# Attention, token choice and expert layers on one core: new layout for the choice's matmuls, moved waits, five operations on GpSimd, one round of key sums folded in

## The chip, the cores and the metric

The program runs on one core of a Trainium2 chip. The metric is the device time of one execution in microseconds (us): the median of three runs. A core has five engines with queues of their own, called here PE (matmuls; its weight loads are shown as PEld), DVE (vector), ACT (scalar), POOL (GpSimd) and SP (here it only starts transfers).

## What is computed

```python
scores = scale * q @ k.T; scores = cap*tanh(scores/cap)        # 8 batches, 12 heads, 448 keys, 64 wide
attn = softmax(scores); x = attn @ v                           # x: 3584 tokens x 768
logits = x @ w_gate                                            # 8 experts
for idx in argsort(-logits.flatten()):                         # greedy, highest logit first
    tok, e = idx // 8, idx % 8
    if assigned[tok] < 0 and counts[e] < 448: assigned[tok] = e; counts[e] += 1
out[assigned == e] = relu(x[assigned == e] @ w1[e]) @ w2[e]    # 768 -> 1024 -> 768
```

All in float32; every expert takes exactly 448 tokens.

## The kernel before, in words

**Attention (`attention`, from the start to about 349 us).** 24 steps g, one for each batch and group of four heads. A step makes scores for 128 keys at a time (`qk`), ACT does tanh and exp, PE multiplies with the values (`av`, `avrem` for the last 64 keys). The row sums of the exponentials, which are needed for the division and for the gate, come from DVE adds over the key tiles (`esum`, L158: parts e1, e2, o1, o2, and r for the last 64 keys) and a matmul with a column of ones (`rnd`, L191). For the last step of the last batch the part r is not added by DVE: four more matmuls (L297) sum the last 64 keys straight from the exponentials. `logit` transposes the gate sums, divides them and keeps the 8 logits of each token.

**Choice (`Routing`).** The greedy choice is done expert by expert: in each of 8 passes the expert that fills up first is found with its 448 tokens. For that, `propose_a` and `propose_b` write each token's best open expert and its logit as three numbers (VA, VB, VC) and a key (K1, K2). `search` then finds the 448th value for each expert: three stages A, B, C (`select`) with 5, 6 and 5 rounds. A round compares 224 proposals with three thresholds (two on DVE, one on ACT), sums the counts with a 4-column matmul (L464), and DVE sets the next thresholds (L468, L471). `finalise` numbers the chosen tokens: `oj` and `oh` are one-hot in the high and low part of the position, `rj` is `oj` times the row number, and four matmuls (L581) with `oh` as weights put every row number in its place. DVE folds the result (`ek`, `ev`), a small matmul (L588) spreads it, and `idx` is what the gather reads. The first pass runs with no other work but the last transposes of attention's result (L37, multiplied by the reciprocal row sums on POOL, L45, and written to `xs` in memory). The other passes run between the matmuls of the experts.

**Experts (`ffn_all`).** For each of 8 experts: `gather` asks for 448 rows of `xs` in four transfers (L721, POOL), PE transposes them (`tx`, L728, for expert 0; `xtr`, L737, for the others, six blocks at fixed places in the expert before), ACT and DVE split them in a high and a low part, and PE does the first layer (L766: 8 groups f of 18 matmuls, 144 in all) and the second (L793: 176). 320 matmuls are one expert. Each of these 320 is a *tick*. The choice is a Python generator whose `yield n` says after how many ticks its next piece is put into the engines' queues; a negative number names a place counted from the start. The queues are in order, so a piece put in too early makes the matmuls behind it wait. `s.hA` is the distance from the compares to the matmul L464, `s.hB` the one from L464 to the next compares. PE is kept working by `warm` matmuls (128x128, results not used) while the first gather is under way: 18 of them after L588 of the first choice, and four between the transposes.

Of the kernel before, what the change touches and what calls it, by code (L numbers as in the profile page):

```python
# [17 lines left out]
def attention(nc, tc, c1, xp, pM, q, k, v, cap, w_gate, xs, L1, ident, on_logits, on_turn, NDEF, xd, setup):  # L18
# [3 lines left out]
    B,H,S,D=q.shape  # L22
# [29 lines left out]
    with ExitStack() as ctx:  # L52
# [228 lines left out]
        g=N-1; b=B-1  # L281
        rnd(b,rB[1][0],False,False); rnd(b,rB[1][1],False,True)
        logit_in(b)
        av(g,0,2); av(g,1,0)
        esum(g,'o1')
        part=logit(b,0,2,final=False)
        esum(g,'o2')
        av(g,1,1)
        avrem(g)
        av_out(g,0)  # L290
        av(g,1,2)
        rnd(b,rB[2][0],True,False)
        av_out(g,1)
        ps=misc[b]
        for gt,kind,a,h in rB[2][0]:
            o,t=h//2%2,h%2; w=64*(t^o)
            nc.tensor.matmul(ps[gt*32:gt*32+32,:S],ones[w:w+64,a,:],ev(g,6)[w:w+64,o,:],start=False,stop=False)  # L297
        rnd(b,rB[2][1],False,True)
# [7 lines left out]
TA=0  # L306
EW=1; WT=4
FMAX=3.4028234e38
class Routing:
# [4 lines left out]
    def setup(s):  # L314
# [23 lines left out]
        nc.gpsimd.tensor_copy(s.e8m,s.e8c)  # L338
        s.ihi=t("ihi",[CP,16,NC],I16)
        nc.gpsimd.iota(s.ihi,[[1,16],[0,NC]],base=0,channel_multiplier=0)  # L340
        s.ilo=t("ilo",[CP,28,NC],I16)
# [55 lines left out]
    def propose_a(s,L,c0,c1):  # L397
# [13 lines left out]
        v.tensor_tensor(w("VA"),w("P"),bc(w("At")),op=ALU.mult)  # L411
    def propose_b(s,c0,c1,parts=(0,1,2,3)):
        T=s.T; n=c1-c0; v=s.nc.vector
        w=lambda k:T[k][:,c0:c1]
        bc=lambda a:a.unsqueeze(2).broadcast_to([112,n,8])
        for x in parts:
            if x==0:
                v.tensor_scalar(w("b"),w("u"),10,4095,op0=ALU.arith_shift_right,op1=ALU.bitwise_and)
                v.tensor_scalar(w("c"),w("u"),1023,None,op0=ALU.bitwise_and)
            if x==1:  # L420
                v.tensor_scalar(w("Bt"),w("b"),-2048.0,2.0**-12,op0=ALU.add,op1=ALU.mult)
                v.tensor_scalar(w("Ct"),w("c"),1024.0,2.0**-22,op0=ALU.add,op1=ALU.mult)
            if x==2:
                v.tensor_tensor(w("VB"),w("P"),bc(w("Bt")),op=ALU.mult)
                v.tensor_tensor(w("VC"),w("P"),bc(w("Ct")),op=ALU.mult)
            if x==3:
                v.tensor_tensor(w("K1"),w("At"),w("Bt"),op=ALU.add)
                v.scalar_tensor_tensor(w("K2"),w("kk"),2.0**-25,w("Ct"),op0=ALU.mult,op1=ALU.add)
    def psum(s):
# [19 lines left out]
    def select(s,wp,Vt,ab,mid=None,post=None):  # L449
        nc=s.nc; v=nc.vector  # L450
        NV=s.NV; steps=s.steps[ab]; H=s.H[ab]; C=s.C[ab]
        th=[s.T0[ab][:,k:k+1] for k in range(3)]
        for i in range(steps):
            cd=s.cds[s.nd%3]; s.nd+=1
            o=wp.tile([128,s.NX],BF16,name="cmpA",bufs=1)
            with nc.allow_low_precision(reason="integers up to 256 are exact in bfloat16"):
                for k in range(s.na,3): nc.scalar.activation(o,Vt,AF.Sign,bias=th[k],scale=-1.0,accum_out=cd[:,k:k+1])
                for k in range(s.na):
                    o=wp.tile([128,NV],BF16,name="cmpD",bufs=2)
                    with s.tc.issue_after(s.hold) if s.hold else nullcontext(): v.tensor_scalar(o,Vt[:,:NV],th[k],None,op0=ALU.is_lt,op1=ALU.add,accum_out=cd[:,k:k+1])  # L460
            if mid and i<len(mid): mid[i]()
            s.pos='A'; yield s.hA; s.pos=''
            ps=s.psum()
            nc.tensor.matmul(ps[:,:4],s.bo,cd,start=True,stop=True)  # L464
            if post and i==(3 if s.cur==0 else 0): post()
            t0=wp.tile([128,1],F32,name="th",bufs=6)
            fl=wp.tile([128,4],F32,name="fl",bufs=3)
            v.scalar_tensor_tensor(fl,ps[:,:4],s.lim,H[:,i,0:4],op0=ALU.is_le,op1=ALU.mult,accum_out=t0)  # L468
            if i+1<steps:
                nt=wp.tile([128,1],F32,name="nt",bufs=2)  # L470
                v.tensor_scalar(H[:,i+1,3:6],C[:,i+1,:],t0,None,op0=ALU.add,op1=ALU.add,accum_out=nt) if ACF else v.tensor_scalar(H[:,i+1,3:6],C[:,i+1,:],t0,None,op0=ALU.add)  # L471
                th=[t0,H[:,i+1,4:5],H[:,i+1,5:6]]
            if i==steps-1:
                s.tA=t0
                if ab=="C": s.row(s.tA)
            s.pos='B'; yield s.hB; s.pos=''
    def search(s,wp,turned=()):
        nc=s.nc; v=nc.vector
        post=None
        if turned:  # L480
            for h in range(s.NC//16):
                if ("VA",h) not in turned: s.turn("VA",h)
            late=[lambda x=x: s.propose_b(s.NC-4,s.NC,(x,)) for x in range(4)]
            post=lambda: s.flips(s.pm.tile([128,512],F32,name="psM"))
        else: late,post=s.turns()
# [58 lines left out]
    def finalise(s,wp,L,update):  # L544
# [26 lines left out]
        v.tensor_tensor(oj,s.ilo,hi[:,1,:].unsqueeze(1).broadcast_to([112,28,NC]),op=ALU.is_equal)  # L571
        oh=s.oh=wp.tile([112,16,NC],F16,name="oh",bufs=1)
        v.tensor_tensor(oh,s.ihi,hi[:,0,:].unsqueeze(1).broadcast_to([112,16,NC]),op=ALU.is_equal)
        rj=wp.tile([112,28,NC],F16,name="rj",bufs=1)
        v.tensor_tensor(rj,oj,s.idc.unsqueeze(1).broadcast_to([112,28,NC]),op=ALU.mult)
        yield 18
        ps=s.psum()
        oc=oh.rearrange("p r c -> p (r c)")
        G=NC//8
        for g in range(G):  # L580
            nc.tensor.matmul(ps[:,:224].rearrange("p (j k) -> p j k",k=8),oc[:,g::G],rj[:,:,g::G],start=(g==0),stop=(g==G-1))  # L581
        ek=wp.tile([128,28,8],F16,name="ek",bufs=1); ev=wp.tile([128,28],F16,name="ev",bufs=1)
        v.tensor_tensor(ek,ps[:,:224].rearrange("p (j k) -> p j k",k=8),s.mk.unsqueeze(1).broadcast_to([128,28,8]),op=ALU.mult)
        with nc.allow_low_precision(reason="one term of each sum is not zero"):
            v.tensor_reduce(ev,ek,axis=AX.X,op=ALU.add)
        yield 4
        ps=s.psum()
# [7 lines left out]
        if update:  # L595
          with s.tc.issue_after(mark.ins) if s.cur==0 else nullcontext():
            z=wp.tile([112,1],F32,name="zz")
            v.tensor_scalar(z,rj[:,0,0:1],0.0,None,op0=ALU.mult)
            v.scalar_tensor_tensor(gt,m[:,0,:],z,m[:,1,:],op0=ALU.add,op1=ALU.add)
# [27 lines left out]
def ffn_all(nc, tc, ctx, rt, xs, w1, w2, out, ident, E, wp, deferred, xctx, gen):  # L627
# [125 lines left out]
    def ffn1(p,f,work):  # L753
# [160 lines left out]
```

## Time and profile before

| | |
|---|---|
| median of 3 runs | 939.32 us (938.67 to 940.23) |
| the profiled execution | 939.89 us, of which the span is 938.1 us |
| PE busy | 898.5 us, 96% of the span |
| DVE, ACT, POOL busy | 586.3, 574.1, 345.2 us |
| end of attention / first expert matmul / last expert matmul starts | 349, 399.2, 929.8 us |

A PE that is busy for 96% bounds the kernel, but a busy PE is not one at its peak: in the last matmuls of a stage it works at one of two clocks, and matmuls with results that nobody uses count as busy. So the shares are read by stage, and in each stage the wait that ends last.

### The profile page before, as it was taken

To read this page: it belongs to the slowest core of one execution; us is meant where nothing else is said; L and a number is where in the kernel's file an instruction comes from. 1 tells how busy PE (TensorE), PEld (TensorE's weight loads), DVE (VectorE), ACT (ScalarE), POOL (GpSimd) and SP (SyncE) were. 2 spreads that over 40 slices of the span, in tenths; PEclk is the share of its full clock that TensorE was granted. 3 is DMA by queue.
4 is the path that set the end of the run, shared out by engine and by line. 5 is a ranking of instruction groups with operands and counts; after the bars stand their busy time and mean duration, and the time that the engine had idled before them with its cause. 6 is when DMAs were issued, how large, how long until landed. Compare 5 with 4: busy or idle time off the path is not lost.

```text
span 938.1 us, 16367 instructions
## 1 busy us (share of the span) xinstructions
PE 898.5 (96%) x5770; PEld 619.8 (66%) x5770; DVE 586.3 (62%) x1980; ACT 574.1 (61%) x795; POOL 345.2 (37%) x469
## 2 busy tenths in 40 slices
PE   5899999999999996799999999999999999999996
PEld 1223333333323235688889989989989989999996
DVE  4779797989888767766665666656656654231210
ACT  6999898999999947274373472562662651532520
POOL 5100000000000007573483493392492683764831
PEclk9999999999999999799999999999999999999998
DMA  8677775856785006760921814516417407426301
GB/s 136 116 142 130 153 136 123 145 121 122 189 166 98 1 20 238 215 211 1 317 71 45 298 46 137 212 41 195 161 32 228 144 18 245 144 57 232 99 9 50
DMA packets 291699, 123.01 MB, mean 131 GB/s; under 512 B 224768, under 2 KB 275712, under 8 KB 291104
## 3 DMA queue, kind: packets, MB, share of 16 engines
q1 hardware_dynamic: 285104, 99.70, 42.7%
q0 software_dynamic: 4656, 22.02, 6.5%
q8 instruction: 45, 0.74, 0.3%
q10 hardware_dynamic: 1856, 0.23, 0.2%
q14 instruction: 38, 0.31, 0.1%
HBM read 97.15 MB, written 24.77 MB: 130 GB/s over the span
## 4 chain that ended last, share of the span: by engine, by line
PE 77%; issue 8%; ACT 5%; POOL 4%; DVE 4%; DMA 2%; ACTq 0%; POOLq 0%; DVEq 0%
PE psH L766 22%; PE psH L793 19%; PE psA L172 11%; PE psS L144 11%; PE psM L191 4%; ACT e L150 3%; PE psS L149 2%; DMA xg<-xs,idx 2%; PE psX L737 2%; PE psA L179 2%; PE psM L37 1%; ACT e L154 1%; DVE cmpD L460 1%; POOL out_dram L778 1%; POOL xn L45 1%
## 5 line engine op out<-in xcount | busy, mean ns | idle before, releaser
L793 PE MATMUL psH<-w2h,hh 128*128 128x384 f32 x896 | 249.5, 344 | 0.0
L793 PE MATMUL psH<-w2l,hh 128*128 128x384 f32 x512 | 175.1, 342 | 0.0
L150 ACT ACTIVATE e<-psS,s 128x896 f32<-128x896 f32 x168 | 161.0, 1000 | 20.4 <-PE psS L144 12.6
L793 PEld LDWEIGHTS psH<-w2h,hh 128*128 128x128 f32 x896 | 163.1, 189 | 0.8
L154 ACT ACTIVATE e<-e,bias,capt 128x1792 f32<-128x1792 f32 (+2 forms) x74 | 154.2, 2083 | 2.5
L45 POOL TENSOR_TENSOR xn<-raw,rin 112x512 f32<-112x512 f32 x24 | 24.4, 1048 | 323.5 <-ACT raw L42 321.7
L766 PE MATMUL psH<-xgh,w1h 128*128 128x448 f32 x384 | 142.6, 371 | 0.3 <-ACT xgh L742 0.3
L766 PE MATMUL psH<-xgh,w1l 128*128 128x448 f32 x384 | 142.3, 371 | 0.0
L766 PE MATMUL psH<-xgl,w1h 128*128 128x448 f32 x384 | 142.1, 370 | 0.0
L144 PE MATMUL psS<-tq,tk 64*64 64x448 f32 x1152 | 127.8, 559 | 9.0 <-DVE rcap L229 6.0
L172 PE MATMUL psA<-e,nv 128*64 128x448 f32 x576 | 124.1, 552 | 0.0
L698 POOL TENSOR_TENSOR w2l<-w2r,w2h 128x768 fp32r<-128x768 f32 x64 | 117.8, 1841 | 12.8 <-ACT w2h L694 12.8
L698 POOL TENSOR_TENSOR w1l<-w1r,w1h 128x768 fp32r<-128x768 f32 x62 | 114.0, 1840 | 20.1 <-ACT w1h L694 15.5
L158 DVE TENSOR_TENSOR es<-es,e 128x896 f32<-128x896 f32 (+1 forms) x94 | 101.9, 1084 | 1.9
L773 DVE SCALAR_TENSOR_TENSOR hh<-psH,hh 128x64 fp32r<-128x64 f32 (+1 forms) x128 | 44.1, 387 | 93.6 <-ACT hh L771 93.2
L799 ACT ACTIVATE on<-psH 128x384 f32<-128x384 f32 x48 | 23.6, 491 | 122.4 <-PE psH L793 122.4
L793 PEld LDWEIGHTS psH<-w2l,hh 128*128 128x128 f32 x512 | 96.7, 189 | 0.0
L172 PEld LDWEIGHTS psA<-e,nv 128*64 128x64 f32 x576 | 34.9, 136 | 83.8 <-issue 69.2
L144 PEld LDWEIGHTS psS<-tq,tk 64*64 64x64 f32 x1152 | 37.0, 134 | 80.1 <-issue 48.8
L766 PEld LDWEIGHTS psH<-xgh,w1h 128*128 128x128 f32 x384 | 72.5, 189 | 5.9 <-ACT xgh L742 0.5
L766 PEld LDWEIGHTS psH<-xgh,w1l 128*128 128x128 f32 x384 | 72.5, 189 | 5.3
L771 ACT ACTIVATE hh<-psH 128x448 fp32r<-128x448 f32 x64 | 34.8, 543 | 67.3 <-PE psH L766 63.1
(255 smaller groups left out, 1256.6 us busy)
## 6 DMA issues: line engine op xcount, KB each, us to landing
w1r<-in_moe_w_dram SPq DMA_DIRECT2D x64, 384.0 KB, 3.7
w2r<-in_moe_w_dram SPq DMA_DIRECT2D x32, 768.0 KB, 7.5
k<-in_k_dram SPq DMA_DIRECT2D x92, 112.0 KB, 2.8
q<-in_q_dram SPq DMA_DIRECT2D x92, 112.0 KB, 2.9
nv<-in_v_dram SPq DMA_DIRECT2D x72, 128.0 KB, 3.0
xs<-xn SPq DMA_DIRECT2D x4, 1344.0 KB, 7.0
xs<-xn SPq DMA_DIRECT2D x4, 896.0 KB, 5.2
xd<-xT SPq DMA_DIRECT2D x2, 1344.0 KB, 6.3
```

The lines of the kernel that those rows point to most:

```text
L45: (nc.gpsimd if late else nc.vector).tensor_tensor(xn[b][:,:,h0:h0+3:2,:],src, rin[b][:,:,2*p:2*p+2].unsqueeze(3).broadcast_to([CP,NJ,2,D] ...
L144: for c in range(2): nc.tensor.matmul(ps[c*64:c*64+64,h,:S],tks[g,0][hp,o,u*128+c*64:u*128+c*64+64],tks[g,1][hp,o,:],start=True,stop=True)
L150: nc.scalar.activation(ev(g,r),ps[:,:,:S],AF.Tanh,scale=s1)
L154: nc.scalar.activation(e,e,AF.Exp,scale=capt,bias=bias)
L158: t=es_t[g]; add=lambda o,a,b: nc.vector.tensor_tensor(o,a,b,op=ALU.add)
L172: nc.tensor.matmul(avp[g,o][h*64:h*64+64,:S],z[:,j,HG*h+o,:],ev(g,3*o+j)[:,h,:],start=(j==0),stop=(o==1 and j==2 and op is None))
L191: nc.tensor.matmul(ps[g*32:g*32+32,:S],lhs,rhs,start=first,stop=last)
L698: (eng or nc.gpsimd).tensor_tensor(view(l),r,view(h).bitcast(F32),op=ALU.subtract)
L766: nc.tensor.matmul(ps[:,:C],a[:,c,:],b[:,c,:],start=(m==0),stop=(m==DC*3-1)); m+=1
L771: nc.scalar.activation(h[:,:C],ps[:,:C],AF.Relu)
L773: nc.vector.scalar_tensor_tensor(h[:,d:d+b-a],ps[:,a:b],0.0,h[:,a:b].bitcast(F32),op0=ALU.max,op1=ALU.subtract)
L793: nc.tensor.matmul(ps[:,:HD],h[:,f,a:a+128],spl[p,2,hf,f//2][w][:,f%2,:],start=(m==0),stop=(m==nm-1))
```

## The change

Six groups of edits.

- Row sums of the last step: o1 and o2 are added ahead of `logit_in`, r is added by DVE too, ahead of `logit`, and the four matmuls L297 go; the second copy of attention's result (`av_out(g,1)`) is issued ahead of the sums' matmuls.
- The fields b and c of a proposal are computed in `propose_a`. The rest of `propose_b` for the last four columns of the first pass goes to POOL, in the first round of stage A, where DVE did it two operations at a time in four rounds; only K2 stays on DVE, in the third round.
- The choice's matmuls: `oh` and the index table are laid out as 4 groups x 16 x 8, so that the 128 weights of a matmul are neighbours in memory, where they were every fourth element; the moving columns are runs of eight neighbours instead of every fourth element. The row number is multiplied into the weights (`oi`, 512 elements) instead of into `oj` (896).
- `yield 8` in place of `yield 4` ahead of the matmul L588.
- During the second pass (`s.cur==1`) the distance from compares to L464 is 8 ticks, or, for less than 20 ticks after the end of a first-layer group, 12 less those ticks and at least 6. It was 7. The first compares of that pass stand at tick 16 instead of 18.
- 12 warm matmuls after the first choice instead of 18.

```diff
         rnd(b,rB[1][0],False,False); rnd(b,rB[1][1],False,True)
+        esum(g,'o1')
+        av(g,0,2); av(g,1,0)
+        esum(g,'o2')
         logit_in(b)
-        av(g,0,2); av(g,1,0)
-        esum(g,'o1')
+        esum(g,'r')
         part=logit(b,0,2,final=False)
-        esum(g,'o2')
         av(g,1,1)
         avrem(g)
         av_out(g,0)
         av(g,1,2)
+        av_out(g,1)
         rnd(b,rB[2][0],True,False)
-        av_out(g,1)
-        ps=misc[b]
-        for gt,kind,a,h in rB[2][0]:
-            o,t=h//2%2,h%2; w=64*(t^o)
-            nc.tensor.matmul(ps[gt*32:gt*32+32,:S],ones[w:w+64,a,:],ev(g,6)[w:w+64,o,:],start=False,stop=False)
         rnd(b,rB[2][1],False,True)
...
+        v.tensor_scalar(w("b"),w("u"),10,4095,op0=ALU.arith_shift_right,op1=ALU.bitwise_and)
+        v.tensor_scalar(w("c"),w("u"),1023,None,op0=ALU.bitwise_and)
+    def propose_b(s,c0,c1,v=None):
+        T=s.T; n=c1-c0; v=v or s.nc.vector
...
+        v.tensor_scalar(w("Bt"),w("b"),-2048.0,2.0**-12,op0=ALU.add,op1=ALU.mult)
+        v.tensor_scalar(w("Ct"),w("c"),1024.0,2.0**-22,op0=ALU.add,op1=ALU.mult)
+        v.tensor_tensor(w("VB"),w("P"),bc(w("Bt")),op=ALU.mult)
+        v.tensor_tensor(w("VC"),w("P"),bc(w("Ct")),op=ALU.mult)
+        v.tensor_tensor(w("K1"),w("At"),w("Bt"),op=ALU.add)
+        if v is s.nc.vector: s.key(c0,c1)
+    def key(s,c0,c1):
+        w=lambda k:s.T[k][:,c0:c1]
+        s.nc.vector.scalar_tensor_tensor(w("K2"),w("kk"),2.0**-25,w("Ct"),op0=ALU.mult,op1=ALU.add)
...
-            s.pos='A'; yield s.hA; s.pos=''
+            s.pos='A'; yield max(6,12-s.since()) if s.cur==1 and s.since()<20 else s.hA+1*(s.cur==1); s.pos=''
...
-            late=[lambda x=x: s.propose_b(s.NC-4,s.NC,(x,)) for x in range(4)]
+            late=[lambda: s.propose_b(s.NC-4,s.NC,PB(nc)),lambda: None,lambda: s.key(s.NC-4,s.NC)]
...
-        oh=s.oh=wp.tile([112,16,NC],F16,name="oh",bufs=1)
-        v.tensor_tensor(oh,s.ihi,hi[:,0,:].unsqueeze(1).broadcast_to([112,16,NC]),op=ALU.is_equal)
-        rj=wp.tile([112,28,NC],F16,name="rj",bufs=1)
-        v.tensor_tensor(rj,oj,s.idc.unsqueeze(1).broadcast_to([112,28,NC]),op=ALU.mult)
+        G=NC//8
+        wide=lambda t: t.rearrange("p (g k) -> p g k",k=8).unsqueeze(2).broadcast_to([112,G,16,8])
+        oh=wp.tile([112,G,16,8],F16,name="oh",bufs=1)
+        v.tensor_tensor(oh,s.ihi,wide(hi[:,0,:]),op=ALU.is_equal)
+        oi=wp.tile([112,G,16,8],F16,name="oi",bufs=1)
+        v.tensor_tensor(oi,oh,wide(s.idc),op=ALU.mult)
         yield 18
         ps=s.psum()
-        oc=oh.rearrange("p r c -> p (r c)")
-        G=NC//8
         for g in range(G):
-            nc.tensor.matmul(ps[:,:224].rearrange("p (j k) -> p j k",k=8),oc[:,g::G],rj[:,:,g::G],start=(g==0),stop=(g==G-1))
+            nc.tensor.matmul(ps[:,:224].rearrange("p (j k) -> p j k",k=8),oi[:,g].rearrange("p r k -> p (r k)"),oj[:,:,g*8:g*8+8],start=(g==0),stop=(g==G-1))
...
-        yield 4
+        yield 8
         ps=s.psum()
         s.selmm=nc.tensor.matmul(ps[:,:28],s.sel,ev,start=True,stop=True)
...
+    rt.warm=warm; rt.since=lambda: now[0]-end[0]
...
+        end[0]=now[0]
         h=hh[p][:,f,:]
         nc.scalar.activation(h[:,:C],ps[:,:C],AF.Relu)
...
-    WG=3; NW=18; WJ=4
+    WG=3; NW=12; WJ=4
...
-    hint[0]=18
+    hint[0]=16
     tx(0,4)
```

Three places show what moves in the queues.

DVE at the end of attention, before (es: row sums, e: exponentials, lg: gate sums, xT: attention's result):

```order
L158 TENSOR_TENSOR es<-es,e_3106 128x896
L195 COPY lg<-psM 128x448
L158 TENSOR_TENSOR es<-e_3106,e_3138 128x896
L208 RECIPROCAL rg_3194<-psM 112x32
L215 TENSOR_TENSOR lt_3196<-psM,rg_3194 112x256
L223 TENSOR_REDUCE lt_3198<-lt_3196 112x4x8
L224 COPY rin<-rg_3194 112x4x4x2
L158 TENSOR_TENSOR es<-es,e_3138 128x896
L184 COPY xT<-psA 128x448 x2
```

and with the change:

```order
L158 TENSOR_TENSOR es<-es,e_3106 128x896
L158 TENSOR_TENSOR es<-e_3106,e_3138 128x896
L158 TENSOR_TENSOR es<-es,e_3138 128x896
L195 COPY lg<-psM 128x448
L158 TENSOR_TENSOR es<-es,e_3138 64x2x448
L158 TENSOR_TENSOR es<-es,e_3138 64x896
L208 RECIPROCAL rg_3197<-psM 112x32
L215 TENSOR_TENSOR lt_3199<-psM,rg_3197 112x256
L223 TENSOR_REDUCE lt_3201<-lt_3199 112x4x8
L224 COPY rin<-rg_3197 112x4x4x2
L184 COPY xT<-psA 128x448 x2
```

Two adds stand ahead of the copy L195 now, and two half adds (64 partitions each) are new behind it. On PE, four matmuls fewer stand behind the copies L184.

PE in the choice of expert 1, before (the second layer of expert 0 runs around it; hh: its input, ev: the folded row numbers):

```order
L581 LDWEIGHTS oh
L581 MATMUL psR<-rj,oh 128x224
L581 LDWEIGHTS oh
L581 MATMUL psR<-rj,oh 128x224
L793 MATMUL psH<-w2h,hh 128x384
L793 MATMUL psH<-w2l,hh 128x384
L793 MATMUL psH<-w2h,hh 128x384
L793 MATMUL psH<-w2l,hh 128x384
L588 LDWEIGHTS r_sel
L588 MATMUL psR<-ev,r_sel 128x28
```

and with the change:

```order
L576 MATMUL psR<-oj,oi 128x224
L789 MATMUL psH<-w2l,hh 128x384
L789 MATMUL psH<-w2h,hh 128x384
L789 MATMUL psH<-w2l,hh 128x384
L789 MATMUL psH<-w2h,hh 128x384
L789 MATMUL psH<-w2l,hh 128x384
L789 MATMUL psH<-w2h,hh 128x384
L789 MATMUL psH<-w2l,hh 128x384
L789 MATMUL psH<-w2h,hh 128x384
L583 LDWEIGHTS r_sel
L583 MATMUL psR<-ev,r_sel 128x28
```

Eight expert matmuls instead of four stand between the two. Counted in ticks of the whole program, L581 moves from 224 to 217 and L588 from 228 to 225 for expert 1; for the experts 2 to 7, L588 moves from 531, 834, 1139, 1459, 1779 and 2099 to 532, 839, 1146, 1463, 1783 and 2103. The first transposes of the gathered rows stay at 292, 604, 900, 1220, 1540, 1860 and 2180.

POOL in the first search, before (xn: attention's result times the reciprocal row sums; gw, xg: tiles of the gate and the gather):

```order
L359 TENSOR_SCALAR r_qm<-r_qi 128x32
L117 COPY gw<-wgs 64x8 x24
L45 TENSOR_TENSOR xn<-raw,rin 112x4x2x64 x24
L715 MEMSET xg 64x768
L721 DMA xg<-xs,idx 128x768 x3
```

and with the change:

```order
L117 COPY gw<-wgs 64x8 x24
L45 TENSOR_TENSOR xn<-raw,rin 112x4x2x64
L415 TENSOR_SCALAR r_Bt<-r_b 112x4
L416 TENSOR_SCALAR r_Ct<-r_c 112x4
L417 TENSOR_TENSOR r_VB<-r_P,r_Bt 112x32
L418 TENSOR_TENSOR r_VC<-r_P,r_Ct 112x32
L419 TENSOR_TENSOR r_K_257<-r_At,r_Bt 112x4
L45 TENSOR_TENSOR xn<-raw,rin 112x4x2x64 x23
L710 MEMSET xg 64x768
L716 DMA xg<-xs,idx 128x768 x3
```

Five small operations stand between the first and the second of the 24 multiplications that `xs` waits for.

## Rows read from the trace of the kernel before

**Rows 1.** Windows by stage; stretch: us, busy us per engine, PEclk, DMA share, GB/s.
```profile
349.10:399.20 50.10, 36.95 (x255) 31.27 (x253) 37.01 (x213) 23.58 (x60) 30.38 (x32) 0.83 0.70 224
399.20:930.20 531.00, 526.69 (x2939) 482.01 (x2939) 270.93 (x1328) 236.97 (x493) 296.30 (x324) 1.00 0.40 131
```

**Rows 2.** Timeline, end of attention (start us, us, engine, line, operation).
```profile
341.41 0.62 DVE L195 COPY lg<-psM 128x448 f32<-128x448 f32 x1 [1.96 <-PE psM L191]
...
346.08 1.15 DVE L184 COPY xT<-psA 128x448 f32<-128x448 f32 x2
...
347.11 0.96 PE L297 MATMUL psM<-e,ones 64*32 64x448 f32 x8
```

**Rows 3.** Instructions of line L158: duration ns min/median/max.
```profile
L158 DVE TENSOR_TENSOR es<-es,e x94: 1050/1085/1095, 16.2 to 345.1; 128x896 f32<-128x896 f32 x48, 64x896 f32<-64x896 f32 x46
```

**Rows 4.** Chain of waits, first search (start us, us, what).
```profile
356.13 0.68 DVE r_Bt L421
```

**Rows 5.** Timeline, GpSimd, first search.
```profile
354.73 3.06 POOL L45 TENSOR_TENSOR xn<-raw,rin 112x512 f32<-112x512 f32 x3 [3.38 <-ACT raw L42]
```

**Rows 6.** Instructions of line L370, small GpSimd operations.
```profile
L370 POOL TENSOR_SCALAR r_T0A<-r_kv x1: 182/182/182, 8.3 to 8.3; 128x3 f32<-128x3 f32 x1
```

**Rows 7.** Timeline, from the first choice's end to the first expert.
```profile
387.27 7.03 PE L653 MATMUL psX<-ident 128*128 128x128 f32 x36
...
388.26 1.21 POOL L721 DMA_INDIRECT xg<-xs,idx  x1 [1.58 <-DVE zz L598]
...
392.35 0.42 DVE L411 TENSOR_TENSOR r_VA<-r_P,r_At 112x256 f16<-112x256 f16 x1
...
396.00 0.60 POOL L681 COPY w1r<-xg 1x1 f32<-1x1 f32 x1 [2.44 <-DMA xg<-xs,idx]
...
398.51 0.38 PE L728 MATMUL psH<-ident,xg 128*128 128x128 f32 x2
```

**Rows 8.** Windows in the same stretch, with the granted clock.
```profile
389.00:393.00 4.00, 4.00 (x21) 4.00 (x21) 3.83 (x18) 1.06 (x2) 3.09 (x4) 0.50 0.88 235
393.50:398.60 5.10, 5.10 (x49) 5.06 (x48) 2.70 (x7) 0.00 (x0) 0.90 (x4) 1.00 0.41 144
```

**Rows 9.** Timeline, TensorE, search rounds under expert 0.
```profile
410.21 0.18 PE L464 MATMUL psR<-r_cd,r_bo 128*128 128x4 bf16 x1 [0.27 <-DVE cmpD L460]
...
422.50 0.18 PE L464 MATMUL psR<-r_cd,r_bo 128*128 128x4 bf16 x1 [0.27 <-DVE cmpD L460]
...
434.75 0.18 PE L464 MATMUL psR<-r_cd,r_bo 128*128 128x4 bf16 x1 [0.52 <-DVE cmpD L460]
```

**Rows 10.** Timeline, TensorE, choice of expert 1 and four flips.
```profile
448.25 0.98 PE L581 MATMUL psR<-rj,oh 112*128 112x224 f16 x4
...
448.90 0.51 PE L793 MATMUL psH<-w2h,hh 128*128 128x384 f32 x1
...
449.59 0.33 PE L793 MATMUL psH<-w2l,hh 128*128 128x384 f32 x1
...
450.14 0.19 PE L588 MATMUL psR<-ev,r_sel 128*128 128x28 f16 x1 [0.21 <-DVE ev L585]
...
460.97 0.26 PE L438 MATMUL psV<-r_id,r_VB 112*128 112x112 f16 x2
...
461.14 0.60 PE L793 MATMUL psH<-w2h,hh 128*128 128x384 f32 x2
```

**Rows 11.** Chain of waits, gathers of experts 1, 3 and 6.
```profile
455.05 9.15 DMA xg<-xs,idx
...
585.51 7.51 DMA xg<-xs,idx
...
779.19 14.16 PE psH L793 x81
```

**Rows 12.** Timeline, GpSimd, last request of expert 6's gather.
```profile
784.05 1.13 POOL L721 DMA_INDIRECT xg<-xs,idx  x1 [0.30 <-issue]
```

**Rows 13.** Gathered tile, expert 6: time from request to landing.
```profile
DMA to landing us min/median/max: 7.4/8.1/8.9
```

More of the change, by code (lines that the diff above doesn't have):

```diff
@@ L306 @@
 TA=0
-EW=1; WT=4
+EW=1; WT=4; PB=lambda nc: nc.gpsimd
 FMAX=3.4028234e38
@@ L338, in setup @@
         nc.gpsimd.tensor_copy(s.e8m,s.e8c)
-        s.ihi=t("ihi",[CP,16,NC],I16)
-        nc.gpsimd.iota(s.ihi,[[1,16],[0,NC]],base=0,channel_multiplier=0)
+        s.ihi=t("ihi",[CP,NC//8,16,8],I16)
+        nc.gpsimd.iota(s.ihi,[[0,NC//8],[1,16],[0,8]],base=0,channel_multiplier=0)
         s.ilo=t("ilo",[CP,28,NC],I16)
@@ L411, in propose_a @@
         v.tensor_tensor(w("VA"),w("P"),bc(w("At")),op=ALU.mult)
-    def propose_b(s,c0,c1,parts=(0,1,2,3)):
-        T=s.T; n=c1-c0; v=s.nc.vector
+        v.tensor_scalar(w("b"),w("u"),10,4095,op0=ALU.arith_shift_right,op1=ALU.bitwise_and)
+        v.tensor_scalar(w("c"),w("u"),1023,None,op0=ALU.bitwise_and)
+    def propose_b(s,c0,c1,v=None):
+        T=s.T; n=c1-c0; v=v or s.nc.vector
         w=lambda k:T[k][:,c0:c1]
         bc=lambda a:a.unsqueeze(2).broadcast_to([112,n,8])
[L416 to L428, printed above, removed]
+        v.tensor_scalar(w("Bt"),w("b"),-2048.0,2.0**-12,op0=ALU.add,op1=ALU.mult)
[7 more added lines that the diff above has]
+        s.nc.vector.scalar_tensor_tensor(w("K2"),w("kk"),2.0**-25,w("Ct"),op0=ALU.mult,op1=ALU.add)
     def psum(s):
@@ L597, in finalise @@
             z=wp.tile([112,1],F32,name="zz")
-            v.tensor_scalar(z,rj[:,0,0:1],0.0,None,op0=ALU.mult)
+            v.tensor_scalar(z,oi[:,0,0,0:1],0.0,None,op0=ALU.mult)
             v.scalar_tensor_tensor(gt,m[:,0,:],z,m[:,1,:],op0=ALU.add,op1=ALU.add)
@@ L647, in ffn_all @@
     m=0
-    wu=[None]
+    wu=[None]; end=[-99]
     def warm(n,t=None):
@@ L653, in warm @@
         for _ in range(n): nc.tensor.matmul(t[:,:128],ident,ident,start=True,stop=True)
-    rt.warm=warm
+    rt.warm=warm; rt.since=lambda: now[0]-end[0]
     step()
```

## The prediction

> **What bounds the kernel now.** I read the windows by stage first. From 399 to 930 us PE is busy for 526.7 of 531.0 us at full clock; from 349.1 to 399.2, the first choice, it is busy for 37 of 50 us at a mean clock of 0.83 [rows 1]. So there are two kinds of time to win. In the expert stage a microsecond counts if PE has to wait or does work that isn't an expert's, and the timeline and the chain of waits tell where. Before 399 us one chain of small steps runs through DVE and PE, and each step on it counts whatever the busy shares are. An expert matmul of the second layer takes 14.16/81 = 0.175 us [rows 11]; the shifts by ticks are priced by that.
>
> **The change, part by part.**
>
> *End of attention.* PE leaves out the four matmuls L297, 0.96 us with the pipeline's tail [rows 2]. What is late next are the copies L184 on DVE, at 346.08 [rows 2], behind which the last sums wait. DVE now does two half adds more, 1.08 each as this line's 64-partition forms fall between 1.05 and 1.10 [rows 3], so 2.17 us. Against that it idled 1.96 us ahead of the copy L195 [rows 2], and the adds o1 and o2 now fill that hole. The rest of 0.2 us can move the copies. Gain between 0 and 0.96; I take 0.8, near the row of what goes.
>
> *Five operations on POOL.* On the chain the operation L421 holds the second round for 0.68 us [rows 4], where other rounds have only PE's round trip, about 0.18 for L464 [rows 9] and 0.1 of hand-over. Gain 0.4; the other moved operations ran in that round trip and give nothing. On POOL five small operations cost 0.18 us each at the nearest row [rows 6], 0.9 us, or 1.5 if the 32-column ones take twice that. POOL had idled 3.38 us ahead of its second multiplication [rows 5], and this is their cover. Were it gone, `xs` would be late by at most those 1.5 us; but the gather's first request waited 1.58 us for DVE after POOL was free [rows 7], so nothing comes of it. The two operations put into `propose_a` stand behind VA, while DVE waits for PE. K2 fits in a round trip.
>
> *Matmuls of the choice.* The four L581 hold PE from 448.25 to 448.90, 0.65 us, or 0.73 ns a column at full clock. Four flips (L438, the transposes of the proposals: f16, neighbouring weights and columns) go from 460.97 to 461.14, 0.17 us for 4 x 112 columns or 0.38 ns a column [rows 10]. At that rate four L581 take 0.34. So 0 to 0.31 us for each of 7 choices under the experts; I take 0.25, near the flips, as the runs of eight are not quite their case. In the first choice the product is smaller but the weights now wait for it: 0.15, between -0.1 and 0.3.
>
> The Trainium skill, SBUF — State Buffer, section "Door 1: The DMA port swizzle", says that two accesses in the same 16-byte line are enough for full bandwidth. Every fourth f16 is a step of 8 bytes, two in a line; by this rule the old layout cost nothing and this term is 0. The rows of L581 and the flips speak against it, but the two differ in more than the step.
>
> *Row numbers asked for later.* L588 starts 0.55 us after the matmul ahead of it, 449.59 to 450.14 [rows 10], where 0.175 is due: 0.38 us of PE waiting for `ev`. The four added matmuls take 0.7 us, so this wait goes, in all 7 choices. The request comes at 1.89 - 0.25 - 0.38 + 0.7 = 1.96 us after L581's start, hardly later than the 1.89 of before. But the place where PE needs the rows is fixed, so the gather has less cover. By expert:
> - Experts 2, 4, 5 and 7 save 0.38 + 0.25, say 0.6 each: 2.4. The cover shrinks by 1, 7, 4 and 4 ticks.
> - Expert 6: the chain has 81 matmuls and no transfer between L588 and the transposes, which begin at 793.35 [rows 11]. The last request at 784.05 [rows 12] lands 8.1 to 8.9 later [rows 13], at 792.2 to 793.0, a slack of 0.4 to 1.2. It loses 0.7. I take 0.4 of the 0.6.
> - Expert 3 is bound by the landing already, its transfer of 7.51 us stands on the chain [rows 11]. Its L581 comes a tick later, so it loses 0.25.
> - Expert 1 is bound by the landing too, 9.15 us [rows 11]. Here L581 comes 7 ticks earlier, 224 to 217, since the search is shorter: 1.2, less the 0.07 by which the request lags, 1.15. If its wait is shorter than that, only the 0.4 of the stall is left.
>
> *Compare waits.* Under expert 0 PE waits for compares at 410.21, 422.50 and 434.75, idle for 0.27, 0.27 and 0.52 us [rows 9]. These rounds put their compares behind the two DVE operations that end a first-layer group. With the new waits compares go ahead of them, and only the last, across the end of the first layer, keeps about half. Gain 0.8. The rounds are 9 ticks instead of 10, so what is late next is ACT's compare behind a weight split; this bounds the gain at 0 from below.
>
> *Twelve warm matmuls instead of 18.* The 18 are 36 passes, two each, in 7.03 us, 0.195 each, nearly all at a granted clock of 0.50 (1.2 GHz) that holds up to 393; from 393.5 it is 1.00 (2.4 GHz), with 49 passes in 5.1 us, 0.104 each [rows 7, 8]. 24 passes end at 391.95. The flips still wait for VA at 392.77 [rows 7], so PE pauses for 0.8 us. Then come 40 passes: 16 transposes of the gathered rows and 12 warm matmuls. At full clock the third block of rows, landed at 396.0 [rows 7], is the bound: 16 passes behind it end at 397.7, 0.9 us sooner than the 398.6 of before (the last row's start and one pass). At half clock throughout they take 7.8 us from 393.1, 2.3 later. I take a gain of 0.1, as the clock may come up before the pause or only behind it.
>
> **Sum.** 0.8 + 0.4 + 0.15 + 0.1 + 0.8 + 1.15 + 2.4 + 0.4 - 0.25 = 5.95 us off the profiled execution's 939.89: 933.9. The median of the runs is 0.57 lower, which would make it 933.4. I say 933.6.
>
> **Rivals.**
> - *The columns cost nothing.* L581's 0.73 ns a column may come from the hand-over from and to the expert matmuls, since only four stand together; the four flips stand between expert matmuls too, which speaks against it. Then 7 x 0.25 and 0.1 are missing: 935.4. The rule of the Trainium skill cited above gives this case.
> - *The clock stays at its lower level through the transposes.* For it: the six matmuls left out are those in which the clock came up [rows 8], and the pause comes in their place. Against: PE still works 4.7 us without a stop. Costs 2.3 + 0.1: 936.0.
> - *DVE ends attention.* The half adds push the copies by the whole 0.9: 0.8 missing, 934.4.
> - *Slower: the gathers land later than PE comes.* Place: the first transposes (L737) of experts 2 to 7. Asking later puts the requests among the weight loads of the next expert; expert 1, whose gather is in such traffic, lands after 9.15 us, where 3 and 6 take 7.5 to 8.9 [rows 11, 13]. Each landing that is late by d costs d less the slack: d for expert 3, and for the five others d - 0.1, if expert 6's least slack (0.8 in the middle, less 0.7) is taken for all. Together 6d - 0.5. That eats the gain of 5.95 from d = 1.1 on and is 0.2% slower from 1.4; if all land as late against expert 3 as expert 1 does, d = 1.65 and it costs 9.4: 943.0. Against: the request hardly moves in time, and the loads stand where they stood.
> - *It doesn't do what it says.* The orders show every move, so only a size can be missing.
>
> **Chances.** A measurement of this kernel can tell about 0.2% from no change, 1.9 us. The forecast's case 0.55, columns 0.18, clock 0.12, DVE 0.06, slower 0.04, something unseen 0.05. All but the last two stay below 937.4, if columns and clock don't both fail together with another term. Faster by over 0.2%: 0.87; within: 0.09; slower: 0.04. The range reaches down to 931.4 (columns 0.31, a gain of 0.9 at the transposes, expert 6 in full) and up to 937.2, columns and most of the clock's price together.
>
> **What would show it.** Right: the last sums of attention start 0.8 us sooner behind L195; no 0.7 on the chain in the second round; four L581 in about 0.4 us; no wait ahead of the matmul of `ev` in the experts; expert 1's gather asked for over 3 us sooner. Wrong: transposes of expert 0 at a clock of 0.50; L737 waiting for transfers in three or more experts; an L581 that still takes 0.65 us.

## Result and the profile after

The changed kernel takes 929.23 us in the median (928.34 to 929.89, 4 runs), the one before 939.33 beside it: a ratio of 0.9891, 95% interval 0.9874 to 0.9908, so 10.1 us faster. The forecast was 933.6, its range 931.4 to 937.2: the sign is right, the size too small by 4.4 us, and the time lies below the range. The profiled execution took 929.69 us.

The page of the changed kernel, its head and first part, then the stages of [rows 1] as windows (stretch: us, busy us per engine, PEclk, DMA share, GB/s), cut at its own first expert matmul:

```profile
span 927.9 us, 16317 instructions
...
PE 893.8 (96%) x5750; PEld 618.3 (67%) x5750; DVE 586.5 (63%) x1977; ACT 574.0 (62%) x795; POOL 346.5 (37%) x474
```
```profile
349.10:396.11 47.01, 35.76 (x239) 30.08 (x236) 35.53 (x208) 23.23 (x60) 31.03 (x37) 0.82 0.74 235
396.11:920.00 523.89, 522.15 (x2939) 480.87 (x2939) 269.98 (x1328) 237.21 (x493) 296.45 (x324) 1.00 0.41 134
```

Three us went ahead of the first expert matmul and seven behind it, where PE is as full as before: what went is work and waiting that isn't an expert's. The timelines tell where, when the same matmul of both kernels is set side by side (start in us; the gain is from the start of the span on):

| matmul | before | after | gained so far |
|---|---|---|---|
| last passes of attention's last value sums (L179) | 344.41 | 344.85 | -0.44 |
| first flip of the first search (L438, now L433) | 353.00 | 352.42 | 0.58 |
| last sum of the first search (L527, L522) | 380.50 | 378.67 | 1.83 |
| first choice's row numbers (L588, L583) | 387.22 | 385.10 | 2.12 |
| first expert matmul, expert 0 | 399.20 | 396.11 | 3.09 |
| ... expert 1 | 471.35 | 464.51 | 6.84 |
| ... expert 2 | 539.09 | 531.48 | 7.61 |
| ... expert 3 | 606.56 | 598.69 | 7.87 |
| ... expert 4 | 673.71 | 664.87 | 8.84 |
| ... expert 5 | 740.60 | 731.02 | 9.58 |
| ... expert 6 | 806.30 | 796.00 | 10.30 |
| ... expert 7 | 870.28 | 860.07 | 10.21 |
| last expert matmul | 929.81 | 919.60 | 10.21 |

The first row is an offset of the two executions: it is there from the first matmuls on. Against it the end of attention gained 1.02.

Timeline of TensorE in the changed kernel, choice of expert 1, which answers [rows 10]:

```profile
442.16 0.34 PE L789 MATMUL psH<-w2h,hh 128*128 128x384 f32 x1
442.34 0.56 PE L576 MATMUL psR<-oj,oi 112*128 112x224 f16 x4
442.67 0.42 PE L789 MATMUL psH<-w2l,hh 128*128 128x384 f32 x1
442.93 0.34 PE L789 MATMUL psH<-w2h,hh 128*128 128x384 f32 x1
...
444.16 0.19 PE L583 MATMUL psR<-ev,r_sel 128*128 128x28 f16 x1
444.20 0.42 PE L789 MATMUL psH<-w2l,hh 128*128 128x384 f32 x1
```

I call *hold* what a foreign group costs PE: from the start of the expert matmul ahead to the start of the second one behind it, less 0.174 us for each of the two in between (0.203 in the first layer). Here it is 442.93 - 442.16 - 0.35 = 0.42. In the kernel before it was 449.24 - 448.07 - 0.35 = 0.82, from these two lines around the group of [rows 10]:

```profile
448.07 0.34 PE L793 MATMUL psH<-w2l,hh 128*128 128x384 f32 x1
...
449.24 0.34 PE L793 MATMUL psH<-w2l,hh 128*128 128x384 f32 x1
```

The hold of the matmul of the row numbers fell from 0.50 to 0.13. Both pairs of numbers repeat in all seven choices within 0.01.

What PE waits for from 396 us to the end, first the kernel before, then the changed one (us in total, times, longest):

```profile
PE psR L464 <- DVE cmpD L460: 1.8, 4, 0.8
PE psR L588 <- DVE ev L585: 1.4, 7, 0.2
PE psX L737 <- DMA xg<-xs,idx: 0.7, 2, 0.5
```
```profile
PE psX L732 <- DMA xg<-xs,idx: 1.0, 2, 0.6
PE psX L732 <- issue: 0.4, 1, 0.4
...
PE psR L459 <- DVE cmpD L455: 0.2, 1, 0.2
```

The waits for `ev` are gone, those for compares nearly so, and those for gathered rows have grown. The first transposes of an expert hold PE 0.44 us when the rows are there. For expert 1, which was late before too, the hold fell from 1.62 to some 1.0; for expert 3 it rose from 0.71 to 1.27, and for expert 7 from 0.44 to 1.29. Three late experts are what the prediction named as a sign of being wrong. Expert 3 is as late in the other runs whose requests stand at the same ticks, expert 7 at most 0.2. So part of the gain was given back.

One group of waits was in nobody's reckoning. Before, the search for expert 2 starts like this (timeline of all engines, kernel before):

```profile
456.38 1.25 POOL L778 DMA_INDIRECT out_dram<-on,idx  x1 [0.30 <-issue]
...
456.99 2.62 DVE L427 TENSOR_TENSOR r_K<-r_At,r_Bt 112x32 f32<-112x32 f16 x1
...
457.69 1.86 POOL L698 TENSOR_TENSOR w1l<-w1r,w1h 128x768 fp32r<-128x768 f32 x1
...
460.93 0.18 PE L464 MATMUL psR<-r_cd,r_bo 128*128 128x4 bf16 x1 [0.77 <-DVE cmpD L460]
...
464.25 0.33 PE L737 MATMUL psX<-ident,xg 128*128 128x128 f32 x1 [0.54 <-DMA xg<-xs,idx]
```

A key sum that takes 0.18 us elsewhere took 2.62 and ended 0.06 after POOL's weight split; the first compares came late by it, and PE was held 0.93 us longer than in the like round of the changed kernel (1.23 against 0.30), where the sum takes 0.18 again. But no time went with it: the last block of expert 1's rows landed at 464.20 (455.05 and 9.15 [rows 11]) and PE turned it at 464.25, so without the 0.93 PE would have waited that much longer there. The changed kernel asks for this block at 449.09 and turns it at 457.36:

```profile
449.09 1.02 POOL L716 DMA_INDIRECT xg<-xs,idx  x1 [0.30 <-issue]
...
457.36 0.33 PE L732 MATMUL psX<-ident,xg 128*128 128x128 f32 x1 [0.44 <-issue]
```

On what this sum waited: the Trainium skill, SBUF — State Buffer, section "Who interferes with whom", says that a DVE instruction with two inputs in SBUF contends with a GpSimd instruction that reads SBUF, that the one issued first holds the port, and that the other is blocked until it has ended. Two operations of the changed kernel agree, of which this is one (the other stands at 759.60):

```profile
693.23 1.84 POOL L693 TENSOR_TENSOR w2l<-w2r,w2h 128x768 fp32r<-128x768 f32 x1 [0.27 <-ACT w2h L689]
...
693.39 1.73 DVE L529 SCALAR_TENSOR_TENSOR qq<-r_K,wA,r_K 112x32 f32<-112x32 f32 x1
```

It takes 0.24 elsewhere; here it starts 0.16 behind the split and ends 0.05 behind it. The key sum agrees in part: it has two such inputs and ends with the split, but it starts 0.70 ahead of it, while POOL issues an indirect transfer (456.38), beside which the product ahead of it, with two such inputs too, ran in its usual 0.42. Why the split that came later went first is not shown.

### The profile page after: what moved, and what is told of

The parts are those of the page before. It is cut to its first block, busy times and chain, and to the rows that moved or that the text cites. A ratio compares the mean times of both kernels' runs of the same rounds, so it can differ in the third digit from the quotient of the medians.

```text
span 927.9 us, 16317 instructions
## 1 busy us (share of the span) xinstructions
PE 893.8 (96%) x5750; PEld 618.3 (67%) x5750; DVE 586.5 (63%) x1977; ACT 574.0 (62%) x795; POOL 346.5 (37%) x474
## 4 chain that ended last, share of the span: by engine, by line
PE 80%; issue 8%; ACT 5%; POOL 3%; DMA 2%; DVE 2%; SPq 0%; POOLq 0%; ACTq 0%; DVEq 0%
PE psH L761 23%; PE psH L789 21%; PE psA L172 11%; PE psS L144 10%; PE psM L191 4%; ACT e L150 3%; PE psS L149 2%; PE psX L732 2%; PE psA L179 2%; PE psM L37 1%; DMA xg<-xs,idx 1%; ACT e L154 1%; PE psL L37 1%; POOL out_dram L774 1%; POOL w1l L693 1%
## 5 line engine op out<-in xcount | busy, mean ns | idle before, releaser
L158 DVE TENSOR_TENSOR es<-es,e 128x896 f32<-128x896 f32 (+1 forms) x96 | 104.1, 1085 | 2.0
L761 PEld LDWEIGHTS psH<-xgl,w1h 128*128 128x128 f32 x384 | 72.5, 189 | 5.1
```

What stands on the lines that cost most here:

```text
L158: t=es_t[g]; add=lambda o,a,b: nc.vector.tensor_tensor(o,a,b,op=ALU.add)
```

## Experiments

Where a run's effect is under 1 us its trace decides: four runs of one kernel lie up to 2.1 us apart, and the kernel before, measured beside each group of runs, came to 938.8 to 939.3.

**The choice's matmuls, one side at a time.** Both sides at the old step (the two operands of L576; the tables go back to the layout that fits):

```diff
-oi[:,g].rearrange("p r k -> p (r k)"), oj[:,:,g*8:g*8+8]
+oi.rearrange("p r c -> p (r c)")[:,g::G], oj[:,:,g::G]
```


> The changed kernel with only the columns put back: weights and moving data of the four matmuls of a choice are taken at every fourth column again. In the trace of the changed kernel these four and the two expert matmuls behind them hold PE 0.42 us longer than the expert matmuls alone would, in the one of before 0.82. Theory (the step between columns costs): 7 times 0.40 under the experts and 0.1 in the first choice, 2.9 us more than the changed kernel's 929.2, so 932.1, and a hold of 0.82 in every choice. Rival, the size of the forecast: 0.25 each, 931.0. Rival, two hits in a 16-byte line are enough (the Trainium skill, SBUF, Door 1): no change, 929.2, and the hold stays at 0.42.

931.56 us (ratio to before 0.9925, 0.9911 to 0.9938), 2.3 more than the changed kernel; the hold is 0.82 in all seven choices. Then the moving data alone, and the weights alone, the other side being stored in an order of columns that fits:

> The changed kernel with only the moving data of the choice's four matmuls at every fourth column again; their weights lie together, in an order of columns that fits. Theory (the moving data sets the pace: with the step the four start 0.200 us apart, without it 0.096, which is 0.89 and 0.43 ns for each of 224 columns): 0.200 apart and a hold of 0.82 in each choice, and the 2.3 us that both sides together cost: 931.5. Rival (the weights cost it): 0.096 apart, hold 0.42, 929.2. Rival (each costs half): hold 0.62, 930.4.

> The changed kernel with only the weights of the choice's four matmuls at every fourth column again; the moving data lies together, in an order of columns that fits. Theory (the moving data sets the pace): 0.096 to 0.11 us apart, hold 0.42 to 0.47, 929.2 to 929.5, weight loads of 0.12 instead of 0.10 beside the matmuls. Rival (the weights cost it): 0.200 apart, hold 0.82, 931.5. Rival (each costs half): hold 0.62, 930.4.

932.08 (0.9926, 0.9912 to 0.9939) and 929.91 (0.9906, 0.9891 to 0.9921). Timelines, choice of expert 1, of these two in that order:

```profile
443.92 0.96 PE L576 MATMUL psR<-oj,oi 112*128 112x224 f16 x4
```
```profile
442.49 0.57 PE L576 MATMUL psR<-oj,oi 112*128 112x224 f16 x4
442.83 0.42 PE L789 MATMUL psH<-w2l,hh 128*128 128x384 f32 x1
443.09 0.34 PE L789 MATMUL psH<-w2h,hh 128*128 128x384 f32 x1
```

With the moving data at a step of four f16 the matmuls start 0.200 us apart (hold 0.81), with the weights alone at that step 0.096 (hold 0.43 to 0.44). So the moving data sets the pace, and all but 0.02 of the 0.40 is its own. That two hits in a 16-byte line are enough, the rule of the Trainium skill that the prediction cites, doesn't hold for the moving data that TensorE reads here; the section's subject is the DMA's ports, it names no reader for this rule, and the runs decide.

**Eighteen warm matmuls again.** The first try also put back the hint behind them, which sets the tick of the first compares under expert 0:

```diff
-WG=3; NW=12; WJ=4
+WG=3; NW=18; WJ=4
...
-    hint[0]=16
+    hint[0]=18
```


> The changed kernel with 18 warm matmuls after the first request instead of 12, and the hint that goes with them. Theory (the warm passes stand in PE's order ahead of the transposes and were the bound there, not the gather): 36 passes from 385.14 in place of 24 end at 391.4 if the clock comes up at 390.6, at 392.2 if it stays at 0.50, so the first transposes start at 391.6 to 392.3 instead of 391.18 and no longer wait for the gather: 0.4 to 1.1 us more than 929.2, so 929.6 to 930.3. Rival, the forecast's reckoning (the gather's landing sets the start with 18 too): within 0.1 of 929.2, and the transposes wait for the transfer as they do now.

935.94 (0.9965, 0.9953 to 0.9977), 6.7 more: neither theory. What PE waits for from 396 us on:

```profile
PE psX L732 <- DMA xg<-xs,idx: 5.1, 7, 1.3
PE psR L459 <- DVE cmpD L455: 1.2, 1, 1.2
```

The hint moves the first round under expert 0 by two ticks; the choice of expert 1 then asks for its rows at tick 232 instead of 225, those of experts 2 to 4 seven ticks later too, and four gathers come late: the transposes of these four experts hold PE 5.4 us longer than in the changed kernel. The key sum took 2.62 again, and again the last rows of expert 1 land behind it. So the warm matmuls were taken back alone:

> The changed kernel with 18 warm matmuls after the first request instead of 12 and nothing else: the hint behind them stays at 16, so that every later step keeps its place among the expert matmuls. Theory (the run before cost 6.7 us since the hint of 18 put the search under expert 0 two ticks later and the choice of expert 1 seven, which takes cover from four gathers; the warm passes themselves cost what lies between the choice's last matmul and the first expert matmul, 11.7 us there against 11.0): 0.7 more than 929.2, 929.9, and the gathers of experts 1 to 4 as in the changed kernel. Rival (the six warm matmuls themselves cost the 6.7, through the clock or the gathers): 935 to 936.

928.95 (0.9896, 0.9881 to 0.9911): nothing lost. The passes (timeline of this run) end at the same time as 24 do in the changed kernel, as the clock came up at 388.3 and not at 390.6:

```profile
384.84 5.93 PE L648 MATMUL psX<-ident 128*128 128x128 f32 x36
390.60 0.26 PE L433 MATMUL psR<-r_id,r_VA 112*128 112x112 f16 x2
...
393.88 0.44 PE L723 MATMUL psX<-ident,xg 128*128 128x128 f32 x2 [0.18 <-DMA xg<-xs,idx]
```

From the choice's last matmul to the first expert matmul the profiles in which the granted clock rose 5.4 to 5.9 us behind the former show 11.7 and 12.0 us with 18 (the first try and the kernel before) and 10.8 to 11.0 with 12; those in which it rose sooner, 11.3 and 11.4 with 18 and 11.0 to 11.7 with 12. So six warm matmuls seem to cost some 0.9 when the clock rises late, from two profiles with 18, and nothing when it rises early: PE then waits for rows, 0.18 in the last line above.

**Late proposals on DVE again** (the line that calls them; `propose_b` takes back its four parts).

```diff
-late=[lambda: s.propose_b(s.NC-4,s.NC,PB(nc)),lambda: None,lambda: s.key(s.NC-4,s.NC)]
+late=[lambda x=x: s.propose_b(s.NC-4,s.NC,(x,)) for x in range(4)]
```


> The changed kernel with the last columns' proposals back on DVE, in four parts between the rounds as before. Theory (beside the stall, DVE's read of what POOL wrote makes 11 later waits on POOL needless, and each such wait costs a step of 0.09 us of its own): 0.4 for the stall of the second round and 0.09 for each of 11 rounds, 1.3 to 1.4 us more than 929.2, so 930.6; the last rounds of the first search take 1.53 us each again, where they take 1.44 now. Rival, the forecast's reckoning (only the stall of 0.4): 929.6, with rounds of 1.44.

930.80 (0.9907, 0.9892 to 0.9923), 1.6 more; from the first flip to the last sum the search takes 27.57 us, 26.25 in the changed kernel, 1.3 more as the theory said. One round of the first search in the changed kernel, then in this run (timeline of DVE and PE):

```profile
368.41 0.18 PE L459 MATMUL psR<-r_cd,r_bo 128*128 128x4 bf16 x1 [0.32 <-DVE cmpD L455]
368.63 0.16 DVE L463 SCALAR_TENSOR_TENSOR fl<-psR,r_HB 128x4 f32<-128x4 f32 x1 [0.27 <-PE psR L459]
368.71 0.08 DVE L463 DVE_READ_ACCUMULATOR fl<-psR,r_HB 128x1 f32 x1
368.83 0.22 DVE L466 TENSOR_SCALAR_CACHE_REDUCE r_HB<-r_CB,th 128x3 f32<-128x3 f32 x1
...
369.85 0.18 PE L459 MATMUL psR<-r_cd,r_bo 128*128 128x4 bf16 x1
```
```profile
368.93 0.18 PE L461 MATMUL psR<-r_cd,r_bo 128*128 128x4 bf16 x1 [0.42 <-DVE cmpD L457]
369.14 0.16 DVE L465 SCALAR_TENSOR_TENSOR fl<-psR,r_HB 128x4 f32<-128x4 f32 x1 [0.27 <-PE psR L461]
369.23 0.08 DVE L465 DVE_READ_ACCUMULATOR fl<-psR,r_HB 128x1 f32 x1
369.44 0.22 DVE L468 TENSOR_SCALAR_CACHE_REDUCE r_HB<-r_CB,th 128x3 f32<-128x3 f32 x1
...
370.46 0.18 PE L461 MATMUL psR<-r_cd,r_bo 128*128 128x4 bf16 x1
```

1.44 against 1.53 us, and the difference is the gap ahead of the table's operation: 0.04 and 0.13. In that gap stands a semaphore instruction: the operation has two waits, for DVE itself and for POOL, which filled the table at the start of the program, and the second wait is an instruction of its own. The trace of before has 13 of them ahead of this operation in the first search, as this run has, that of the changed kernel two. The other eleven, by this account, went since `key` reads what POOL has just made: after that wait everything POOL did earlier is known to be done. To see this by itself, the kernel before got one copy more:

```diff
+            v.tensor_copy(wp.tile([1,1],F32,name="rd"),s.qm[0:1,0:1])
```


> The kernel before with one DVE copy of a single element more, at the start of the first search while DVE waits for PE: it reads a table that POOL wrote last at the start of the program. Theory (once DVE has waited for something that POOL did late, the 13 later waits on POOL's tables, one in each round and with a step of 0.09 us of its own, aren't needed): 13 times 0.087 = 1.1 us less than before, 938.0 to 938.2, rounds of the first search 1.44 instead of 1.53 us, and no step of its own ahead of the threshold sums. Rival (the waits are covered, or they stay): within 0.2 of before, rounds of 1.53.

936.65 (0.9978, 0.9969 to 0.9987), 2.2 less than before, with rounds of 1.44 and none of the 13 steps left. From the first flip to the last sum its search takes 25.68 us, 27.50 before. Of these 1.8 the steps make 1.1; the other 0.7 may be the clock's: this profile shows 1.00 throughout the search, where in the kernel before PE's clock falls to 0.50 from 358.9 to 362.4. What makes up the rest of the 2.2 wasn't followed.

**The compare waits put back.**

```diff
-yield max(6,12-s.since()) if s.cur==1 and s.since()<20 else s.hA+1*(s.cur==1)
+yield s.hA
```


> The changed kernel with the waits between a round's compares and its matmul put back (7 ticks throughout in the search under expert 0). Theory (measured from matmul start to matmul start, five rounds of before held PE 1.98 us longer than the others, now 0.43; the search is also 7 ticks longer, 1.2 us, which comes off the cover of expert 1's gather): 1.55 and up to 1.2 more, 930.8 to 932.0, and 0.9 more still if the key sum on DVE meets a weight split of POOL again as it did before (2.62 us instead of 0.18). Rival, the forecast's size: 0.8 for the waits, 1.2 for the gather, at most 931.2, with idle times of 0.3 to 0.5 in three rounds.

932.47 (0.9933, 0.992 to 0.9947), 3.2 more, in the theory's range with the key sum, but the parts are others. Waits of PE from 396 us on, and the first round of the search for expert 2:

```profile
PE psX L732 <- DMA xg<-xs,idx: 2.5, 4, 0.9
PE psR L459 <- DVE cmpD L455: 1.6, 5, 0.8
```
```profile
451.55 2.61 DVE L419 TENSOR_TENSOR r_K<-r_At,r_Bt 112x32 f32<-112x32 f16 x1
...
455.48 0.18 PE L459 MATMUL psR<-r_cd,r_bo 128*128 128x4 bf16 x1 [0.77 <-DVE cmpD L455]
```

The rounds under expert 0 hold PE only some 0.4 longer than with the new waits, since the hint of 16 has moved them too. But the choices of experts 1 to 4 come five ticks later, so at the transposes of these four the holds are 2.8 us longer. The key sum meets the split again and holds PE 0.93, but here too it is no part of the price: the last rows of expert 1 land at 458.14, behind it, and PE turns them at 458.19.

**Row numbers asked for 4 and 6 ticks behind the choice's matmuls,** instead of 8 (`yield 4`, `yield 6`):

> The changed kernel with the matmul of the row numbers 4 ticks behind the choice's matmuls again instead of 8. Theory (what the choices under the experts pay for a stall that comes back, and what the gathers win by being asked for 4 ticks earlier per choice so far): 7 times 0.37 = 2.6 more for the stall; less up to 0.5, 0.7 and 0.85 by which PE waits for the rows of experts 1, 3 and 7 now: 929.8 to 931.8. Rival, the forecast's reckoning (the waits for rows of experts 3 and 6 hardly depend on it): 2.4 to 2.7 more, 931.6 to 931.9.

> The changed kernel with 6 ticks instead of 8 ahead of the matmul of the row numbers. Theory (the stall at 4 ticks was 0.37 us, 2.1 ticks, so 6 are nearly enough, and the requests of experts 1 to 4 go out 2, 4, 6 and 8 ticks earlier, those of 5 to 7 two): 0.3, 0.7 and 0.35 less wait for the rows of experts 1, 3 and 7, up to 0.1 of stall in each choice: 927.9 to 928.9. Rival (landings follow the traffic and not the request): 929.2 to 929.9. Rival (the new places meet a weight split of POOL): 930 or more, with a DVE operation of 2 us or more in the proposals.

929.17 (0.9898, 0.9883 to 0.9913) and 927.94 (0.9886, 0.9871 to 0.9901). Waits of PE from 396 us on, 4 ticks, then 6:

```profile
PE psR L583 <- DVE ev L580: 1.3, 7, 0.2
PE psR L459 <- DVE cmpD L455: 0.2, 1, 0.2
```
```profile
PE psX L732 <- DMA xg<-xs,idx: 0.3, 1, 0.3
PE psR L459 <- DVE cmpD L455: 0.2, 1, 0.2
```

With 4 the stall is back in seven choices, 2.4 us of holds, and no gather is late any more, 2.3 us less at the transposes: the time is the same. Six ticks leave no stall and little of the late gathers, and the holds of all foreign groups together fall by 1.5 us, from 44.3 in the changed kernel to 42.8.

**The end of attention as before,** the rest as changed:

> The changed kernel with the end of attention as before: the last group's sums in two half adds, and a last round of four key-sum matmuls of its own. Theory (the matmuls are on the path and the third add is covered): 1.0 more, 930.2, the last logits begin 1.0 later behind the turning of the logits. Rival (DVE's two half adds cost what the matmuls save): within 0.2 of 929.2.

929.38 (0.9896, 0.9881 to 0.9911). The theory's step is in the trace: from the sums L191 to the turning of the logits L202 it takes 346.45 to 350.01, 3.56 us, and 346.66 to 349.20, 2.54, in the changed kernel. The first expert matmul starts 0.94 later, at 397.05. In the time of the whole it can't be told: the profiled execution of the changed kernel has a gather for expert 7 that is 0.85 late, this one hasn't.

**The best of it:** 6 ticks, and the early read:

> The changed kernel with 6 ticks ahead of the matmul of the row numbers and the early read of a POOL table at the start of the first search. Theory: the 1.3 us that 6 ticks brought, and 0.17 for the two rounds of the first search that still wait for POOL's tables (the others don't since the last key waits for POOL): 927.6 to 927.9, all rounds without that step. Rival (the read delays the search's first compares by its own 0.1 and the first request stays bound by the gather): 927.9 to 928.1.

926.44 us (925.69 to 927.42), ratio 0.9868, 0.9853 to 0.9884: all its runs lie below those of the changed kernel. It gains 2.8 and not 1.5 (by the ratios, each to the kernel before beside it, 2.2). The view shows no wait of PE for a gather under the experts; from start to start the transposes for expert 3 still take some 0.2 too long. And the clock didn't fall in the search. The window 356.5 to 363.3 us in the changed kernel and in this one:

```profile
356.50:363.30 6.80, 6.20 (x33) 5.43 (x32) 4.96 (x35) 4.95 (x13) 5.83 (x6) 0.50 0.65 205
```
```profile
356.50:363.30 6.80, 4.73 (x39) 3.73 (x40) 5.62 (x39) 5.34 (x16) 5.63 (x7) 1.00 0.65 204
```

The two rounds that start there take 3.99 us at the lower clock and 3.23 at the higher. Of the twelve profiles without the read two stay at 1.00 there; both with it do. Whether that is the read's doing stays open.

## Why the prediction fell short

| step of the prediction | forecast | the two traces | what the runs add |
|---|---|---|---|
| end of attention | 0.8 | 1.02 | 1.02 in the trace of the run |
| five operations on POOL | 0.4 | 1.25 | 1.0 of it are eleven waits that went |
| first choice's matmul and DVE | 0.15 | 0.29 | |
| twelve warm matmuls | 0.1 | 0.97 | 0 to 0.9, by the clock |
| compare waits, expert 0 | 0.8 | 1.55 | five rounds, from start to start |
| expert 1's gather | 1.15 | 2.2 | 1.2 for seven ticks, 0.9 for a shorter transfer |
| experts 2 to 7 | 2.55 | 3.4 | columns 0.40 each, stall 0.37 each, two late gathers |
| offset of the executions | | -0.44 | |

No one step makes up the 4.3 us that the sum lacks against the traces: five terms fell short by 0.75 to 1.05 each.

- *"Compare waits. Gain 0.8"* had its size wrong. I took the idle times of [rows 9]. The idle time counts from the modelled end of the matmul ahead, but the next could have started 0.16 us before that; two more rounds were held 0.21 and 0.23 without any idle time in the view. From start to start the five make 1.98 us, 0.43 in the changed kernel. And I had read the flips at 460.97 [rows 10] without the matmul 0.04 ahead of them, which had waited 0.77: the key sum behind it wasn't seen, though its going gave nothing by itself.
- *"So 0 to 0.31 us for each of 7 choices; I take 0.25"*: the cause was right (the moving side of it), the size 0.40. The flips gave the pace (0.38 ns a column; 0.43 now), but the old cost was more than the 0.65 counted from the first to the next matmul: the expert matmul behind the group took 0.345 where 0.174 is due.
- *"the other moved operations ran in that round trip and give nothing"*: the wait that was to go went. That `key`'s wait for POOL would make eleven others needless wasn't thought of, 1.0 us; the gap of 0.13 in each round is plain in a timeline of DVE.
- *"At full clock ... 0.9 sooner"* was the case that came, 0.97 in the two traces, and I took 0.1 between it and the loss. The rival of the low clock fell: the clock was at 1.00 from 390.6 on, ahead of the first transposes. But 0.97 is this pair of executions, and a kernel with 18 lost nothing.
- *"this wait goes, in all 7 choices"*: it went, 0.37 each for the 0.38 forecast. That it is worth so much fell: with the stall back the time is the same, since with the later requests experts 1, 3 and 7 are late. The rival "gathers land later" was right in mechanism, and its price 2.3 us of holds where it named 9.4.
- *"Expert 1 is bound by the landing too"* was right, and so was its 1.2 for the seven ticks. That bound hides what columns, stall and key sum held PE ahead of the landing: the last request stands 6.75 us behind the choice's first matmul, 6.80 before, so all that went there gave nothing for this expert. But the sum took the transfer as it was, 9.15 us. In the changed kernel the last block is turned 8.27 after its request; in four runs with its hint and its 8 ticks, whose traces show the landing, the transfer takes 8.2 to 8.5, in the kernel before and the one with the early read 9.15 and 9.39. Why it is shorter stays open.

## What to carry over

Read what a small matmul costs a full TensorE from start to start, over the matmul behind it too; idle time leaves out a part. A search that is woven into other work by counted steps has no price of its own: two ticks made four transfers late and put a DVE operation into POOL's way, 6.7 us in all, so after each edit look again at who comes late. Where the path waits for a transfer that is already asked for, a hold ahead of its landing costs nothing: look at what ends last before a wait is priced. And let an engine wait once, early, for the last thing another did at the start, if its short chain reads many tables from there.

## What was new about the hardware

- Moving data in f16 at a step of four halves TensorE's pace, 0.200 against 0.096 us for 224 columns at a granted clock of 1.00; weights at the same step cost 0.01 to 0.02 us of hold.
- A small DVE operation with two inputs in SBUF ended only with a POOL split, after 2.6 us for 0.2 to 0.4, in four of these kernels in the same choice; in each it started ahead of the split, while POOL issued an indirect transfer. Another in the changed kernel took 1.73 for 0.24 behind a split that had started first.
- A second wait of a DVE operation costs 0.09 us, on a chain of rounds of 1.5.
- A wait of PE for rows can cost twice: in the run with the hint of 18 PE waits 1.27 and 0.71 us at 589.5 and 590.6, and then its clock is at 0.50 for three us (windows of that run), which cost some 1.5 us more:

```profile
586.00:591.00 5.00, 3.02 (x20) 2.46 (x19) 0.82 (x4) 1.18 (x4) 1.10 (x2) 1.00 0.89 322
591.60:594.60 3.00, 3.00 (x11) 3.00 (x11) 1.55 (x9) 1.33 (x3) 0.36 (x1) 0.50 0.04 8
```
